# The filter's spectrum made on chip beside the first stage of batch 1, with the second stage lagging 13 steps

## The chip, the core and the metric

The kernel runs on one core of one Trainium2 chip. The metric is the device time of one execution in microseconds; three runs of the kernel before gave 908.36, 910.75 and 912.71, with a median of 910.75.

## What is computed

A causal long convolution by FFT, followed by a mixture of experts with soft slots. Everything is float32.

```python
# x (8, 5696, 128), h (5696, 128), phi (128, 32), w1 (8, 128, 1024), w2 (8, 1024, 128)
Xf = np.fft.rfft(x, n=2 * S, axis=1)
Hf = np.fft.rfft(h, n=2 * S, axis=0)
y  = np.fft.irfft(Xf * Hf[None], n=2 * S, axis=1)[:, :S].reshape(-1, D)
logits = y @ phi
d = softmax(logits, axis=0)                       # over all 45568 tokens
slot_input = (d.T @ y).reshape(E, 4, D)
slot_out[e] = np.maximum(slot_input[e] @ w1[e], 0) @ w2[e]
out = softmax(logits, axis=1) @ slot_out          # (45568, 128)
```

## The kernel before

The sequence of 5696 = 89 x 64 points is transformed by matmuls as a two-dimensional transform of 90 x 64. There are nine sequences: g = 0 is the filter h, g = 1 to 8 are the batches. Each goes through three stages, and DRAM scratch lies between the stages, since a stage needs another axis of the data on the partitions.

- **Stage A** (`stage_a`, lines 230 to 253). `load_x` (178) brings two chunks of 4 + 4 columns into one of two buffers `xc`; `fold` (209, line 217) makes sums and differences of near and far columns on POOL; PE multiplies by the table `s1` (241); ACT copies PSUM to a tile `fst` (243), of which there are four; the DMA that stores `fst` into `f` is kept back in `pending` and issued on SP's queue by `flush` (225). The low 60 frequencies of a chunk are done in every step, the high 30 of two chunks together in every odd step.
- **Stage B** (`stage_b1`, 275 to 314, and `stage_b2`, 316 to 352). A sequence has 12 units (NW). A unit loads a tile `gt` from `f` (`load_g`, 270), multiplies by `wt` on PE into the PSUM tile `bt` (284), and on VectorE multiplies by the filter's spectrum, `Hr` and `Hi` (304, 312). For the filter itself (g = 0) the multiplication is by the table `turn`, and line 308 writes `Hr` and `Hi` instead. `stage_b2` multiplies by `vt` (327) into `bz`, ACT copies to `zst` (332), and the store goes to `zm` or `zr`.
- **Stage C** (`stage_c1` to `stage_c6`, softmax and dispatch, 394 to 563). A pair of chunks T is loaded from `zm` and `zr` (374, 385), transformed by `im` and `ir` (412, 417), folded out, transposed (439), multiplied by phi (448), and taken through both softmaxes; `dispatch` (527) adds to the slots' accumulator.

The order is written by hand: the pools don't schedule. One loop over steps t interleaves the stages, and each engine gets its instructions in the order in which the loop names them. There are NJ = 8 chunks in a sequence. Stage A handles chunk t in step t, the filter in steps 0 to 7 and batch b in steps 8b to 8b + 7 (b from 1), until step 71. `units(t)` gives the stage-B units of a step, one in odd steps and two in even ones, with a lag:

```python
LAG_B, LAG_C = NJ + 1, 3 * NJ + 3      # 9 and 27
```

So filter B is in steps 9 to 16, B of batch 1 in steps 17 to 24, and stage C handles pair T from step 27 + 2T on. The loop ends at step 80 (`last_front`); the remaining pairs, the experts and the output follow in a tail. `prefetch` issues `gt` loads three units ahead. PSUM is split: four banks go round through `bank()`, two belong to `bt` and two to `bz`.

At the start VectorE sets `xc` and the stage-C buffers (176, 359 to 364), and ACT's queue issues the table loads and eight stores of zeros into `zr` (625), before its first copy. On SP's queue stand the filter's first loads, then the tables `wt` and `vt` (618, 619).

Of the kernel before, what the change touches and what calls it, by code (L numbers as in the profile page):

```python
# [11 lines left out]
F32 = mybir.dt.float32  # L12
AF = mybir.ActivationFunctionType
# [5 lines left out]
def transform_tables(S, N1, N2, CH, LOW, MAIN, XR):  # L19

    N, R1, HALF, P = N1 * N2, S // N2, N2 // 2, 2 * N2
    k1 = np.arange(N1)  # L30
    alpha = np.pi * (k1 + 0.5) / N1
    m1 = np.arange(R1) - (N1 - 1) / 2
    a1 = np.outer(m1, alpha)
    part = np.stack([np.cos(a1), -np.sin(a1), -np.cos(a1)], 1)
    s1 = np.zeros((P, 2, 3, N2 + HALF))
    for i, r in enumerate((slice(0, R1), slice(XR - R1, XR))):
        s1[r, i, :, 0:LOW] = part[:, :, 0:LOW]
        s1[r, i, :, N2:N2 + N1 - LOW] = part[:, :, LOW:]
    a0 = np.outer(alpha, np.arange(N1 // 2) + 0.5)
    part = np.stack([np.cos(a0), -np.sin(a0), -np.cos(a0)], 1)  # L40
    NP = N1 // 2
    im = np.zeros((2, MAIN, 2, N2))
    ir = np.zeros((2, 2, HALF, N2))
    for o in range(2):
        for c in range(2):
            im[o, :, c, 0:NP] = part[0:MAIN, o + c]
            ir[o, c, 0:N1 - MAIN, 0:NP] = part[MAIN:, o + c]
    k2 = np.arange(N2)
    omega = np.pi * (k1[:, None] + 2 * N1 * k2[None] + 0.5) / N
    m2 = np.arange(HALF) - (N2 - 1) / 2  # L50
    a2 = m2[None, :, None] * omega[:, None, :]
    w = np.concatenate([np.cos(a2), np.sin(a2)], 1)
    back = np.arange(N2).reshape(2, HALF).T.reshape(-1)
    NU = (NP + 1) // 2
    turn = (N1 - 1) / 2 * alpha[:, None] + (N2 - 1) / 2 * omega
    wq = np.zeros((2, N2, NP, N2))
    vq = np.zeros((2, N2, NU, 2, N2))
    tn = np.zeros((2, N2, 2, (NU + 1) // 2, 2, 2))
    for a in range(2):
        wq[a] = w[a::2].transpose(1, 0, 2)  # L60
        for q in range(NP):
            vq[q % 2, :, q // 2, a] = w[2 * q + a][back].T
            tn[q % 2, :, 0, q // 4, a, q // 2 % 2] = np.cos(turn[2 * q + a]) / N
            tn[q % 2, :, 1, q // 4, a, q // 2 % 2] = np.sin(turn[2 * q + a]) / N
    im, ir, wq, vq, tn = [t.reshape(P, *t.shape[k:]) for t, k in
                          ((im, 2), (ir, 3), (wq, 2), (vq, 2), (tn, 2))]
    return [np.ascontiguousarray(t, dtype=np.float32) for t in (s1, im, ir, wq, vq, tn)]
# [3 lines left out]
def kernel(  # L71
# [47 lines left out]
    t_s1, t_im, t_ir, t_w, t_v, t_turn = [  # L119
        nc.inline_tensor(t, f"tab_{n}").ap()  # L120
        for n, t in zip(("s1", "im", "ir", "w", "v", "turn"),
                        transform_tables(S, N1, N2, CH, LOW, MAIN, XR))]
    fd = [nc.dram_tensor(f"f_{g}", (N1, N2, 2, D), F32, kind="Internal").ap() for g in range(B + 1)]
# [26 lines left out]
    ypool = work.enter_context(tc.tile_pool(name="ypool", bufs=1))  # L150
    front = ExitStack()
# [6 lines left out]
    bpool = front.enter_context(tc.tile_pool(name="bpool", bufs=1))  # L158
# [5 lines left out]
    Hr = fconst.tile([P, NW, 2, 2, D], F32, name="Hr")  # L164
    Hi = fconst.tile([P, NW, 2, 2, D], F32, name="Hi")
# [9 lines left out]
    for t_ in xcs:  # L175
        nc.vector.memset(t_[:, :, :, :], 0.0)

    def load_x(m, halves=((0, 2 * CH),)):
# [3 lines left out]
        g, j = divmod(2 * m, NJ)  # L182
        if g == 0:
            src, blocks = h, ((0, R1 // 16 * 16), (R1 // 16 * 16, R1))
        else:
            r0 = min((g - 1) * R1, B * R1 - XR) * N2
            src, blocks = x.rearrange("b t d -> (b t) d")[r0:r0 + XR * N2], ((0, XR),)
        src = src.rearrange("(a n) d -> a n d", n=N2)
        t_ = xcs[m % len(xcs)]
# [19 lines left out]
    def fold(c):  # L209
        if c not in xs:  # L210
            return
        t_ = xs.pop(c)
        y_ = xf[c % len(xf)]
        i = CH * (c % 2)
        near, far = t_[:, 0, i:i + CH, :], t_[:, 1, ::-1, :][:, i:i + CH, :]
        for o in range(2):
            nc.gpsimd.tensor_tensor(out=y_[:, o, :, :], in0=near, in1=far,  # L217
                                    op=AL.subtract if o else AL.add)
        folded[c] = y_

# [6 lines left out]
    def columns(c, o):  # L227
        return folded[c][:, o, :, :].rearrange("p n d -> p (n d)")

    def stage_a(c, high):  # L230
# [7 lines left out]
        for q in range(2):  # L238
            p = bank()
            for i, (c_, o, m, cols) in enumerate(groups):  # L240
                nc.tensor.matmul(p[i * m:(i + 1) * m, :], s1[:, g // B, q + o, cols], columns(c_, o),  # L241
                                 start=True, stop=True)
            nc.scalar.activation(st[:, :, q, :],  # L243
                                 p[:, :].rearrange("p (n d) -> p n d", d=D), AF.Copy)
        k0, k1 = (LOW, N1) if high else (0, LOW)
        for i, (c_, o, m, _) in enumerate(groups):
            n0 = o * HALF + CH * (c_ % NJ)
            pending.append(partial(
                nc.sync.dma_start,
                out=fd[g][k0:k1, n0:n0 + CH, :, :].rearrange("k n c d -> k (n c d)"),  # L250
                in_=st[i * m:i * m + k1 - k0, :, :, :].rearrange("k n c d -> k (n c d)")))
# [12 lines left out]
    def load_g(u):  # L264
        if u >= (B + 1) * NW:
# [6 lines left out]
            in_=fd[g][8 * w:8 * w + 2 * n].rearrange("(q a) r c d -> (a r) q (c d)", a=2))  # L272
        gs[u] = t_

    def stage_b1(u):
        g, w, us = parts(u)
        t_ = gs.pop(u)
# [18 lines left out]
        for p_, H_ in (((pi[r, 0:k, :, :], turn[:, 1]), (pv, turn[:, 0])) if g == 0 else  # L296
                       ((pi[r, 0:k, :, :], Hi), (pv, Hr))):
            if g:
                h_ = H_[r, w].rearrange("p a o d -> p (a o) d") if m == 2 else H_[r, w, :, 0]
            else:  # L300
                h_ = (H_[r, w].rearrange("p a o -> p (a o)") if m == 2 else H_[r, w, :, 0]).unsqueeze(2)
                h_ = h_.broadcast_to([r.stop, k, D])
            h_ = h_.unsqueeze(2).broadcast_to([r.stop, k, 2, D])
            nc.vector.tensor_tensor(out=p_, in0=pv, in1=h_, op=AL.mult)  # L304
        if g == 0:
            for c, op_, H_ in ((0, AL.add, Hr), (1, AL.subtract, Hi)):
                h_ = H_[r, w, :, :, :].rearrange("p a o d -> p (a o) d") if m == 2 else H_[r, w, :, 0, :]
                nc.vector.tensor_tensor(out=h_, in0=pv[:, :, c, :], in1=pi[r, 0:k, 1 - c, :], op=op_)
            return
# [43 lines left out]
    ybufs = [ypool.tile([P, Q * CH, D + 1], F32, name=f"y{i}") for i in range(2)]  # L353
    zring = [(ypool.tile([P, 2, CH, 2, D], F32, name="zc"), ypool.tile([P, 2, CH, D], F32, name="zx"))]
    lt = ypool.tile([P, CH, 2, HP], F32, name="lt")
    dt = ypool.tile([P, CH, 2, HP], F32, name="dt")
    om, op = [ypool.tile([P, CH, D], F32, name=n) for n in ("om", "op")]
    yt = ypool.tile([D, Q * CH, 2, MH], F32, name="yt")
    nc.vector.memset(zring[0][1][:, :, :, :], 0.0)
    for t_ in (lt, dt):  # L360
        nc.vector.memset(t_[:, :, :, :], 0.0)
    nc.vector.memset(lt[HP:P, :, :, MH - 1:MH], -2.0 ** 127)
    for t_ in ybufs:
        nc.vector.memset(t_[:, :, D:D + 1], 1.0)
# [29 lines left out]
    def stage_c1(T, between=lambda: None):  # L394
        zt, zx = zs.pop(T)
        y_ = ybufs.pop(0)
        ybufs.append(y_)

# [36 lines left out]
    def stage_c2(T):  # L435
        for k in (3, 1, 0, 2) if tail else (3, 2, 1, 0):
# [8 lines left out]
    def stage_c3(T):  # L445
        p = bank()
# [8 lines left out]
    def column_max(T):  # L455
        mx = cpool.tile([P, 1], F32, name="mx", tag="mx")
        nc.vector.reduce_max(out=mx[:, :], in_=lt[:, :, :, 0:MH], axis=AX.XYZ)
# [13 lines left out]
    def stage_c4(T):  # L471

        p = bank()
# [3 lines left out]
        L = ypool.tile([P, Q, CH, NSL], F32, name="L", tag="L", bufs=2)  # L477
# [10 lines left out]
    def stage_c5(T):  # L488
        p = bank()
# [3 lines left out]
        d_ = ypool.tile([P, CH, P], F32, name="d", tag="d", bufs=1)  # L493
# [104 lines left out]
    LAG_B, LAG_C = NJ + 1, 3 * NJ + 3  # L598
# [4 lines left out]
    def units(t):  # L603
        g, i = divmod(t - LAG_B, NJ)
        if t < LAG_B or g > B:
            return []
# [3 lines left out]
    queue = [(u, t) for t in range(steps) for u in units(t)]  # L610
# [4 lines left out]
    load_x(0, ((0, CH), (CH, CH)))  # L615
    nc.scalar.dma_start(out=s1[:, :, :, :], in_=t_s1)
    load_x(1)
    nc.sync.dma_start(out=wt[:, :, :], in_=t_w)
    nc.sync.dma_start(out=vt[:, :, :, :], in_=t_v)
    nc.scalar.dma_start(out=phi[:, :], in_=moe_phi)  # L620
    nc.scalar.dma_start(out=turn[:, :, :, :, :], in_=t_turn)
    nc.scalar.dma_start(out=im[:, :, :], in_=t_im)
    nc.scalar.dma_start(out=ir[:, :], in_=t_ir)
    for i in range(8):
        nc.scalar.dma_start(
            out=zr[i // 4][i // 2 % 2, i % 2, N1 - MAIN:].rearrange("k (j r) d -> (k j) (r d)", r=2 * CH),
            in_=zring[0][1][0:4 * (HALF - N1 + MAIN), :, :, :].rearrange("p h n d -> p (h n d)"))
    fold(0)
    wait_b2 = []

    for t in range(last_front + 1):
# [23 lines left out]
        T, U, V, W, X = [pair(k) for k in (0, 2, 1, 3, 5)]  # L655
        if t < NA:
            stage_a(t, False)
            fold(t + 1)
        if t == last_front:
# [32 lines left out]
        else:  # L692
            if t % NJ == 0:
                prefetch(wait_b2[-1] + AHEAD if wait_b2 else AHEAD - 1)
# [238 lines left out]
```

## Time and profile before

| | |
|---|---|
| median of 3 runs | 910.75 us (908.36 to 912.71) |
| span of the profiled execution | 906.7 us; its own total time is not told, and the runs leave 2 to 6 us around the span |
| busy: PE, PEld, DVE, ACT, POOL | 757.3, 383.0, 601.1, 436.6, 399.9 us |
| DMA | 278.33 MB, mean 307 GB/s |
| `f` stores of all nine sequences | 144 of 240 KB and 144 of 120 KB |
| `gt` loads | 99 of 512 KB and 9 of 128 KB |

The profile is one execution seen by the hardware profiler. Its page shows the span in 40 slices of 22.7 us, one digit for each engine (the busy share in tenths), the clock that the throttle granted to PE, and the share and rate of the 16 DMA engines. "Windows" gives the same sums for stretches that one chooses, "timeline" the instructions in order of time with the idle time ahead of each and what released it, and "groups" the instructions of one line and shape with their busy time, mean duration in ns and idle time ahead. One float32 matmul instruction shows as two records. A row with SPq or ACTq is an instruction of the queue that issues a DMA, not its transfer.

### The profile page before, as it was taken

The page shows a single profiled execution, that of the slowest core. Times are in us where ns is not written, and L with a number is a line of the kernel's source. Part 1 is how long each engine was busy: PE and PEld are TensorE (multiplying, and loading weights), DVE is VectorE, ACT ScalarE, POOL GpSimd, SP SyncE. Part 2 cuts the span into 40 slices and gives each one's busy share as a digit, 9 for nine tenths or more (in the row PEclk, how much of TensorE's full clock was granted, in tenths as well). Part 3 has the DMA queues.
Part 4 walks back from the last instruction along what each step waited for, and adds up shares of the span by engine and source line. Part 5 has one row for each costly group of instructions (what it writes and reads, how often), then busy time and mean ns, then how long its engine had stood idle before and what let it go on. Part 6 is the DMA issues. An engine that isn't in the chain of part 4 may idle for free.

```text
span 906.7 us, 21292 instructions
## 1 busy us (share of the span) xinstructions
PE 757.3 (84%) x8308; PEld 383.0 (42%) x8308; DVE 601.1 (66%) x896; ACT 436.6 (48%) x880; POOL 399.9 (44%) x353
## 2 busy tenths in 40 slices
PE   5867687689989998998999999989888877767893
PEld 2222233234444443444444444435444434344882
DVE  2049876567778776777677787758778766653552
ACT  2423343345655565565556555645544444563441
POOL 4634424245656655655555566645332224651000
PEclk9889999989999999999899999989988888766865
DMA  8999999999999999999999999999988868540798
GB/s 264 314 312 342 321 362 290 307 369 357 320 298 375 347 322 337 353 315 291 360 354 331 312 366 348 324 329 331 294 252 293 267 199 341 186 164 1 296 405 332
DMA packets 170443, 278.33 MB, mean 307 GB/s; under 512 B 13543, under 2 KB 128231, under 8 KB 165135
## 3 DMA queue, kind: packets, MB, share of 16 engines
q1 hardware_dynamic: 169336, 275.74, 89.7%
q8 instruction: 66, 1.08, 0.5%
q10 hardware_dynamic: 1008, 1.25, 0.4%
q14 instruction: 33, 0.27, 0.1%
HBM read 147.94 MB, written 129.00 MB: 305 GB/s over the span
## 4 chain that ended last, share of the span: by engine, by line
PE 41%; DMA 32%; DVE 7%; ACT 7%; issue 6%; POOL 3%; SPq 2%; DVEq 0%; ACTq 0%; POOLq 0%
DMA gt<-f 9%; PE bt L284 8%; PE bank L241 7%; PE bz L327 7%; DMA zx<-zr 5%; DMA zc<-zm 5%; PE bank L412 4%; DMA out_dram<-o 4%; DMA f<-fst 4%; PE bank L417 3%; PE bank L439 3%; PE bank L448 2%; DMA zr<-zst 2%; ACT zst L332 2%; ACT fst L243 2%
## 5 line engine op out<-in xcount | busy, mean ns | idle before, releaser
L241 PE MATMUL bank<-x,s 128*32 128x512 f32 (+1 forms) x1152 | 216.5, 613 | 13.3 <-POOL x L217 8.2
L217 POOL TENSOR_TENSOR x<-xc 128x512 f32<-128x512 f32 x144 | 180.5, 1279 | 96.3 <-PE bank L241 77.8
L430 POOL TENSOR_TENSOR y<-y,op 128x512 f32<-128x512 f32 x64 | 77.6, 1212 | 227.6 <-DVE op L404 225.1
L284 PE MATMUL bt<-gt,wt 64*64 64x256 f32 x1620 | 123.3, 414 | 55.2 <-issue 27.1
L243 ACT ACTIVATE fst<-bank 128x512 f32<-128x512 f32 x216 | 123.0, 592 | 77.1 <-PE bank L241 53.5
L304 DVE TENSOR_TENSOR pi<-bt,Hi 128x1024 f32<-128x1024 f32 x96 | 112.9, 1176 | 65.1 <-PE bt L284 65.0
L332 ACT ACTIVATE zst<-bz 128x1024 f32<-128x1024 f32 x96 | 93.3, 972 | 109.8 <-PE bz L327 93.7
L312 DVE TENSOR_TENSOR yf<-bt,pi 128x512 f32<-128x512 f32 x192 | 119.3, 663 | 3.3
L284 PEld LDWEIGHTS bt<-gt,wt 64*64 64x64 f32 x1620 | 57.7, 140 | 135.7 <-issue 77.1
L304 DVE TENSOR_TENSOR bt<-bt,Hr 128x1024 f32<-128x1024 f32 x96 | 113.0, 1177 | 0.0
L327 PE MATMUL bz<-yf,vt 64*64 64x256 f32 x1440 | 109.3, 403 | 0.0
L241 PEld LDWEIGHTS bank<-x,s 128*32 128x32 f32 (+1 forms) x1152 | 54.0, 125 | 129.2 <-issue 91.3
L404 DVE TENSOR_TENSOR y<-bank,y 128x512 f32<-128x512 f32 x32 | 22.1, 692 | 97.2 <-ACT y L420 96.9
L327 PEld LDWEIGHTS bz<-yf,vt 64*64 64x64 f32 x1440 | 63.6, 143 | 25.4 <-issue 4.2
L512 POOL TENSOR_TENSOR L<-L,rs 128x512 f32<-128x512 f32 x32 | 33.5, 1048 | 87.2 <-DVE rs L511 43.7
L439 PE MATMUL bank<-ident,y 109*128 109x109 f32 x512 | 62.6, 272 | 8.8 <-ACT yt L441 8.8
L504 ACT ACTIVATE L<-L 128x512 f32<-128x512 f32 x32 | 20.2, 630 | 102.6 <-POOL L L501 102.6
L430 POOL TENSOR_TENSOR y<-y,om 128x512 f32<-128x512 f32 x54 | 63.9, 1183 | 2.1
L420 ACT ACTIVATE y<-bank 128x512 f32<-128x512 f32 x32 | 19.1, 596 | 93.0 <-PE bank L417 93.0
L439 PEld LDWEIGHTS bank<-ident,y 109*128 109x128 f32 x512 | 52.6, 148 | 20.4 <-POOL x L217 16.4
L412 PE MATMUL bank<-zc,im 64*64 64x512 f32 x480 | 60.8, 623 | 0.0
L441 ACT ACTIVATE yt<-bank 128x360 f32<-128x360 f32 x128 | 53.0, 483 | 6.2 <-PE bank L439 5.8
(101 smaller groups left out, 861.7 us busy)
## 6 DMA issues: line engine op xcount, KB each, us to landing
gt<-f SPq DMA_DIRECT2D x99, 512.0 KB
f<-fst SPq DMA_DIRECT2D x144, 240.0 KB
zm<-zst SPq DMA_DIRECT2D x128, 256.0 KB
zc<-zm SPq DMA_DIRECT2D x30, 1024.0 KB
xc<-in_x_dram SPq DMA_DIRECT2D x32, 768.0 KB
f<-fst SPq DMA_DIRECT2D x144, 120.0 KB
out_dram<-o SPq DMA_DIRECT2D x16, 1024.0 KB
zx<-zr SPq DMA_DIRECT2D x30, 512.0 KB
```

Source lines behind the costliest of these rows:

```text
L217: nc.gpsimd.tensor_tensor(out=y_[:, o, :, :], in0=near, in1=far, op=AL.subtract if o else AL.add)
L241: nc.tensor.matmul(p[i * m:(i + 1) * m, :], s1[:, g // B, q + o, cols], columns(c_, o), start=True, stop=True)
L243: nc.scalar.activation(st[:, :, q, :], p[:, :].rearrange("p (n d) -> p n d", d=D), AF.Copy)
L284: nc.tensor.matmul(bt[q * HP:(q + 1) * HP, a, o, :], wt[r, 2 * i + q, :], t_[r, 2 * o + q, :, :].rearrange("p c d -> p (c d)"), start=True ...
L304: nc.vector.tensor_tensor(out=p_, in0=pv, in1=h_, op=AL.mult)
L312: nc.vector.tensor_tensor(out=y_[r, 0:k, c, :], in0=pv[:, :, c, :], in1=pi[r, 0:k, 1 - c, :], op=op_)
L327: nc.tensor.matmul(bz[a * HP:(a + 1) * HP, q, o, :], vt[r, i, a, :], y_[r, a * m + o, :, :].rearrange("p c d -> p (c d)"), start=True, sto ...
L332: nc.scalar.activation(st[:, 0:m, 0:n, :].rearrange("p o q x -> p q o x"), bz[:, 0:n, 0:m, :], AF.Copy)
L412: nc.tensor.matmul(ps[o, c][h_ * HP:(h_ + 1) * HP, :], im[r, c, :], zt[r, h_, :, c, :], start=True, stop=False)
L430: eng.tensor_tensor(out=part_, in0=part(v, 0), in1=o_[:, :, :], op=sign)
L439: nc.tensor.transpose(p[:, i * TR:(i + 1) * TR], ys[T][0:TR, k * CH + i, 0:D], ident[0:TR, 0:TR])
L441: nc.scalar.activation(yt[:, k * CH:(k + 1) * CH, :, :], of_tokens(p), AF.Copy)
```

## The change

The filter no longer goes through DRAM. The loop starts at step 8, with stage A of batch 1, and the lags grow: `LAG_B` is 13 and `LAG_C` is 31, so that B of batch 1 is in steps 21 to 28, stage C starts at step 31, and `last_front` is step 84.

- All filter chunks are loaded at the start into buffers of their own (`hx`, in the space that `Hr` and `Hi` take later), on SP's queue among the first three loads of x and ahead of `wt` and `vt`. `fold_filter` makes the sums and differences on VectorE into `hf`, with the column index innermost.
- `filter_a`: 16 groups of 8 features in steps 11 to 16 (3, 3, 3, 3, 2, 2). Each is 32 matmuls with 32 columns of weights from `hf` and a moving table `sh` of 90 columns, into `bt` or `bz` by turns; VectorE copies the odd groups and ACT the even ones to `Fh`, a tile in SBUF.
- Filter B in steps 17 to 20, three units each, reads `Fh` instead of `gt`. ACT makes the products with one part of `turn` (four instructions of 256 elements a unit), and VectorE finishes `Hr` and `Hi` with eight instructions of 128 elements, in place of four instructions of 1024 and 512.
- The stage-C buffers become views of one tile, `ymain`, in the space of `Fh`. `open_y` allocates it at step 21, where POOL now sets it and ACT's queue issues the eight `zr` stores, ahead of that step's stage A.
- Stage A works on 96 partitions (XR) instead of 128, and `xc` is no longer cleared.

```diff
-    Hr = fconst.tile([P, NW, 2, 2, D], F32, name="Hr")
-    Hi = fconst.tile([P, NW, 2, 2, D], F32, name="Hi")
+    hx = [fconst.tile([P, n, 2, 2 * CH, D], F32, name=f"hx{i}", tag=k)
+          for i, (n, k) in enumerate(((3, "Hr"), (1, "Hi")))]
...
+    def fold_filter(c):
+        t_ = xs.pop(c)
+        i = CH * (c % 2)
+        near, far = t_[0:R1, 0, i:i + CH, :], t_[0:R1, 1, ::-1, :][:, i:i + CH, :]
+        for o, op_ in ((0, AL.add), (1, AL.subtract)):
+            nc.vector.tensor_tensor(out=hf[0:R1, o, :, CH * c:CH * c + CH].rearrange("p d n -> p n d"),
+                              in0=near, in1=far, op=op_)
+
+    HG = 2 * CH
+
+    def filter_a(k):
+
+        p = bps.tile([P, 2, 512], F32, name="fh", tag="bz" if k % 2 else "bt")
+        for i in range(HG):
+            for a in range(2):
+                for o in range(2):
+                    g = (2 * a + o) * HALF
+                    nc.tensor.matmul(p[g:g + HALF, i // CH, i % CH * N1:(i % CH + 1) * N1],
+                                     hf[0:R1, o, k * HG + i, :], sh[0:R1, o, a, :],
+                                     start=True, stop=True)
+        src = p[:, :, 0:CH * N1].rearrange("p b (i x) -> p x b i", i=CH)
+        dst = Fh[:, :, :, k * HG:(k + 1) * HG].rearrange("p k c (b i) -> p (k c) b i", b=2)
+        if k % 2:
+            nc.vector.tensor_copy(out=dst, in_=src)
+        else:
+            nc.scalar.activation(dst, src, AF.Copy)
...
-        t_ = gs.pop(u)
+        t_ = gs.pop(u) if g else Fh[:, 4 * w:min(4 * w + 4, NP), :, :]
...
+        if g == 0:
+            blocks = [(a, o) for a in range(2) for o in range(m)]
+            for i, (a, o) in enumerate(blocks):
+                nc.scalar.activation(pi[r, i, :, :], pv[:, i, :, :], AF.Copy,
+                                     scale=turn[r, 1, w, a, o:o + 1])
+            for i, (a, o) in enumerate(blocks):
+                for c, op_, H_ in ((0, AL.add, Hr), (1, AL.subtract, Hi)):
+                    nc.vector.scalar_tensor_tensor(
+                        out=H_[r, w, a, o, :], in0=pv[:, i, c, :], scalar=turn[r, 0, w, a, o:o + 1],
+                        in1=pi[r, i, 1 - c, :], op0=AL.mult, op1=op_)
+            return
...
+    def open_y():
...
+        all_ = ypool.tile([P, n], F32, name="ymain", tag="main")
...
+        nc.gpsimd.memset(yv["zx"], 0.0)
+        for i in range(8):
+            nc.scalar.dma_start(
+                out=zr[i // 4][i // 2 % 2, i % 2, N1 - MAIN:].rearrange(
+                    "k (j r) d -> (k j) (r d)", r=2 * CH),
+                in_=yv["zx"][0:4 * (HALF - N1 + MAIN)].rearrange("p h n d -> p (h n d)"))
+        for k in ("lt", "dt"):
+            nc.gpsimd.memset(yv[k], 0.0)
...
-    LAG_B, LAG_C = NJ + 1, 3 * NJ + 3
+    LAG_B, LAG_C = NJ + 5, 3 * NJ + 7
+    GH = dict(zip(range(NJ + 3, NJ + 9), (3, 3, 3, 3, 2, 2)))
+    UH = {LAG_B + NJ - 4 + i: (3 * i, 3 * i + 3) for i in range(4)}
...
+    load_x(NJ // 2, ((0, CH), (CH, CH)))
+    load_x(0)
+    load_x(NJ // 2 + 1)
+    for m in range(1, NJ // 2):
+        load_x(m)
     nc.sync.dma_start(out=wt[:, :, :], in_=t_w)
     nc.sync.dma_start(out=vt[:, :, :, :], in_=t_v)
...
-    fold(0)
+    fold(NJ)
+    for c in range(NJ):
+        fold_filter(c)
...
-    for t in range(last_front + 1):
+    for t in range(NJ, last_front + 1):
...
+        if t == LAG_B + NJ:
+            open_y()
         if t < NA:
             stage_a(t, False)
             fold(t + 1)
+        for _ in range(GH.get(t, 0)):
+            filter_a(left.pop(0))
+        if t == LAG_B + NJ - 4:
+            assert not left
+            first.close()
+            bpool = front.enter_context(tc.tile_pool(name="bpool", bufs=1))
+        while t < LAG_B + NJ and us:
+            slot_b()
```

## The prediction

> **What bounds the kernel now.** A step is one turn of the loop over t; A is the first stage (lines 241 and 243), B the second (284 to 332), C the rest. I began with the page's slices, which show that the bound differs by stage.
>
> ```profile
> PE   5867687689989998998999999989888877767893
> ...
> PEclk9889999989999999999899999989988888766865
> DMA  8999999999999999999999999999988868540798
> ```
>
> DMA stands at 9 for 28 slices in a row, so the change, which takes away traffic, is aimed at the busiest resource. Next I cut the span into stages with the windows view; the columns are the stretch, its length, busy us of PE, PEld, DVE, ACT and POOL, granted clock, DMA share, GB/s.
>
> ```profile
> 0.00:8.00 8.00, 0.00 (x0) 0.00 (x0) 5.58 (x8) 0.00 (x0) 1.82 (x8) 1.00 0.63 162
> 8.00:43.00 35.00, 29.66 (x128) 9.08 (x128) 0.00 (x0) 13.55 (x23) 21.26 (x18) 0.90 0.95 319
> 43.00:96.00 53.00, 39.55 (x322) 13.65 (x320) 37.01 (x42) 16.40 (x28) 24.82 (x20) 0.94 0.97 324
> 96.00:173.00 77.00, 57.82 (x600) 25.41 (x596) 54.47 (x64) 30.34 (x43) 24.85 (x20) 0.96 1.00 327
> 173.00:663.00 490.00, 449.08 (x5101) 213.85 (x5100) 362.93 (x550) 269.63 (x543) 260.92 (x222) 0.98 0.99 332
> 663.00:747.00 84.00, 66.06 (x768) 37.16 (x760) 63.09 (x97) 36.82 (x75) 27.09 (x24) 0.84 0.79 258
> ```
>
> The rows are: start; A of the filter (steps 0 to 7); B of the filter (8 to 16); B of batch 1 (17 to 26); all stages together (27 to 72); B and C without A (73 to 80). Up to 663 us DMA paces. Without A its share falls to 0.79, yet steps hardly shorten: z loads of steps 25, 57, 65, 73 and 79 are issued at 168.0, 500.8, 583.4, 663.2 and 724.4 us, so a step takes 10.4 us with A ((583.4-168.0)/40) and 10.2 without. There DVE (63 of 84 us) and PE at a 0.84 clock pace. So **DMA taken out late buys almost nothing; what counts is when C starts.** C starts at step 27, at 173.2 us, and in the changed kernel at step 31. The step count from there to the tail is 53 in both. I price the stretch up to C.
>
> **What goes.** Filter A and B through HBM: 5.9 MB written and 5.9 MB read, 8 steps of A, 12 units of filter B at 3.6 us of DVE (two of 1.22, two of 0.69, less overlap; the chain of waits shows them back to back from 73 to 94 us). The loop begins at step 8, and C's step 31 comes 23 steps later instead of 27.
>
> **What comes, step by step.** (1) *Start.* All four filter loads, wt and vt now stand ahead of the first f store. In the kernel before, the fifth fst tile waits for the first to be stored:
>
> ```profile
> 27.52 1.08 ACT L243 ACTIVATE fst<-bank 128x512 f32<-128x512 f32 x2 [7.09 <-DMA f<-fst]
> ```
>
> By then 6,744 KB had been queued (tables 448, zr 768, three filter loads 2,136, wt and vt 2,912, store 480): 260 GB/s counted from 1 us. After, it is 9,172 KB (tables 628, three x loads 2,304, four filter loads 2,848, wt and vt 2,912, store 480), so the store lands at 36 us. The fifth fst tile is step 11's, and in ACT's order it stands ahead of the copy that frees the transform's first bank. PE gets through A of steps 8 to 11 and two groups by about 30 us, then waits; step 11's copies (2 x 0.59), the bank copy (0.77), the third group and the rest of A end it at 41.5 us. fold_filter's 16 DVE operations lie under this: 0.69 each by line 312, 1.3 by line 430 in the tail, 11 to 21 us beside DVE's empty 0 to 43.
>
> (2) *The transform on PE.* 16 groups of 32 matmuls of 32x90, two records each. The nearest row is the dispatch, with weights of the same width and 129 columns, here in the timeline:
>
> ```profile
> 418.98 1.10 PE L527 MATMUL bank<-y,d 128*32 128x129 f32 x32
> ```
>
> That is 34 ns a record back to back; line 852 (128 columns, 128 records in 3.7 us) gives 29. Scaled by columns the floor is 20, unscaled the ceiling 34; I take 26, near the short row, since issue doesn't shrink with columns: 64 x 26 = 1.65 us a group (1.3 to 2.2). The Trainium skill ("TensorE: Matmul & The Clock Gate", section "Wait — 56ns, not 53.3ns?") gives a start-to-start floor of about 25 ns however short the matmul, by which a group would be 1.6 us; no row of this trace has so short a matmul in that form. Copies out (720 elements, between 592 and 1025 ns on ACT by lines 243 and 332, 690 and 1222 on DVE by lines 308 and 304) run under the next group, by the two tags. If that cover were gone they would add 16 x 0.85 = 14 us. Steps 12 to 16 hold seven blocks of A at 1.87 us and 13 groups: 13.1 + 21.5 = 34.6. After PE's long wait the first work runs at half clock, as before (a bt block takes 1.98 instead of 1.09 us at 669.8, after 3.08 us idle): +2. Step 17 then starts at **78 us** (70 to 88).
>
> (3) *Filter B, steps 17 to 20.* Twelve units from the chip: 8 matmuls (1.09 us), four ACT scalings of 256 elements, eight DVE operations of 128.
>
> ```profile
> L332 ACT ACTIVATE zst<-bz 128x256 f32<-128x256 f32 x8 | 3.1, 383 | 3.0 <-PE bz L327 2.1 <-DMA f<-fst 0.9
> ...
> L532 DVE SCALAR_TENSOR_TENSOR acc<-acc,dn,bank 128x129 f32<-128x129 f32 x31 | 8.3, 268 | 3.4 <-PE bank L527 3.4
> ```
>
> DVE: 92 x 0.26 = 24 us; ACT: 46 x 0.38 = 17.5. Two banks alternate, so a step's third unit waits until DVE is done with the first: 0.5 of ACT and 2.1 of DVE after that one's matmuls, less the second unit's 1.1 meanwhile, leave 1.5 of PE waiting. PE: six blocks of A 11.2, units 12.5, waits 4 x 1.5: **30 us** (26 if DVE never pauses, 36 if ACT's fst copies hold the scalings). DMA needs only 14 (4 x 1.1 MB), so it can't be what paces. Step 21 starts at 108. It does what step 17 did, which began at 95.6:
>
> ```profile
> 95.55 1.94 PE L241 MATMUL bank<-x,s 128*64 128x512 f32 x8
> ...
> 173.15 1.94 PE L241 MATMUL bank<-x,s 128*64 128x512 f32 x8
> ```
>
> So **+12.5 us**. The ten steps from there to C move the same bytes at a DMA share of 1.0, 77.6 us in both.
>
> (4) *open_y at step 21.* Memsets on POOL ahead of fold(22) are hidden (about 3 us; the fold is needed some 8 us later). The eight zr stores stand in ACT's queue ahead of step 21's fst copies; they took 7.77 us at 6.2 us, and now the first waits for the memset and others for gt and x landings. Behind them wait fst, hence PE's banks, hence f and z stores. PE has some 5 us of other work: +4 (0 to 8).
>
> (5) *The rest.* fold and A's matmuls over 96 partitions: durations go by the free size, nothing. Four steps of C lose A: 4 x 0.2 = -1. The stage-C buffers become views of one tile; stage C waits on nearly the same engines at each instruction in the two built programs: nothing. One w1 load is repeated (0.5 MB, beside a DMA share under 0.8): nothing.
>
> Sum: 12.5 + 4 - 1 = **+15.5**. The profiled span is 906.7; its own total isn't told, but the runs (908.36 to 912.71) leave 2 to 6 us around it, so I add to the median: 910.75 + 15.5 = 926.
>
> **Rivals.** *DMA paces the head too* (ends faster). If copies and matmuls hide, bytes set step 21: first loads 8.9 MB, six more x loads 4.7, f stores of 13 steps 9.3, three gt 1.6: 24.5 MB at 315 GB/s and 2 us of start are 80 us against 95.6, so 895. It decides if steps 11 to 20 average under 4.5 us; A alone takes 2.8 on PE. For it: the 0.95 share from 8 to 43. Against it: three groups add 5 us to a step whose bytes need 3.5. Beside it the Trainium skill ("Perfetto Trace Analysis", section "Identifying the Most-Contended Engine") says to improve the most-contended engine, which is DMA here. 0.17. *The pieces cancel*: groups at 1.3 us, units at 26, no stall at step 21, a start stall 6 us shorter: 15.5-4-4-4-6 gives 908; 0.10. *Views of one tile order stage C*: 1 us in each of 32 pairs gives 958; for it, one name where twelve were, against it the equal waits: 0.05. *The transform runs at half clock*: there the dispatch takes 1.83 us for 32 records (673.4 us), 57 ns each; 16 x 64 x 31 ns is 32 us more, 958; it needs waits between the groups long enough to drop the clock; against it, stage A lies between them: 0.04. The same page and section of the Trainium skill gives 62 ns a matmul where the sequencer decodes in microcode, by which the sum would be some 37 us more; the rows at 29 and 34 ns speak against that. My forecast holds 0.64.
>
> **Chances and range.** About 0.5% (4.6 us) is what a measurement of this kernel can tell from no change. Faster 0.17, same 0.10, slower 0.73. The forecast's own bounds add to 908 and 945 (groups +7, units +6, stall +4, +2 of start); to leave out no more than 0.2 I reach down to 902.
>
> **What would show it.** Right: PE idle near 30 to 38 us; 26 ns a record; step 21's A near 108 us; a hole in PE and ACT just after; C from about 189; steps of 10.4 us later. Wrong: step 21 before 96 us (the DMA rival), stage-C pairs over 21 us (the views), or steps without A under 9.5 us, which would make the removed traffic worth something late.

## The result, and the profile after

| | before | after |
|---|---|---|
| median of 4 runs | 911.39 us (908.36 to 912.71) | 935.03 us (934.22 to 939.0) |
| ratio after / before | | 1.0267 (95%: 1.0232 to 1.0302) |
| span of the profiled execution | 906.7 us | 933.7 us (its own time is 935.59) |
| DMA | 278.33 MB | 267.35 MB |

The change made the kernel 2.7% slower, though it moves 11 MB less. Single runs of the kernels below spread by up to 36 us, and the longer ones show a lower granted clock in their records; ratios leave the disturbed runs out.

These are the slices of after's page, as the prediction showed them for before (PE's clock and the DMA share):

```profile
PE   5598768767997999999799989999778877667893
...
PEclk9679888997999999999999989999888888878865
DMA  9955389999999999999999999999789848460698
```

The change shows in the first six digits of the DMA line: 9 9 5 5 3 8, where before had 8 and then 9s. From there on the two lines are much alike. The windows view of after cuts that stretch finer. Its columns are the stretch, its length, busy us of PE, PEld, DVE, ACT and POOL, then granted clock, DMA share and GB/s:

```profile
25.00:50.00 25.00, 15.02 (x220) 8.68 (x223) 7.43 (x9) 4.31 (x7) 5.94 (x5) 0.59 0.87 285
50.00:75.00 25.00, 23.50 (x674) 17.43 (x676) 4.54 (x5) 8.46 (x13) 6.48 (x6) 0.87 0.52 145
75.00:100.00 25.00, 19.92 (x348) 9.18 (x336) 9.36 (x31) 14.88 (x32) 9.95 (x8) 0.93 0.55 147
100.00:125.00 25.00, 17.81 (x138) 6.36 (x140) 16.64 (x64) 13.88 (x33) 4.10 (x5) 0.79 0.49 150
```

From 50 to 125 us DMA works at half its share and PE is busy, or waits at a low clock. Nothing that was taken off DMA can shorten this stretch.

I read the time by the start of a step, which is the start of its first matmul of stage A:

| | before | after | forecast of after |
|---|---|---|---|
| step 12 (after only) | | 46.3 | 41.5 |
| step 17 of after | | 82.7 | 78 |
| batch 1 enters B (before's step 17, after's 21) | 95.6 | 123.2 | 108 |
| C starts (before's step 27, after's 31) | 173.2 | 203.0 | 189 |
| from there to the end of the span | 733.6 | 730.7 | 1 less |

So +27.7 us in the head, +2.1 in the ten steps up to C, and -2.8 in all the rest give the +27.0 between the spans. The medians differ by 23.6.

**The start**, in after's timeline (line 246 is `filter_a`, 276 stage A's matmul, 254 ACT's copy to `Fh`, 278 the copy to `fst`, 234 the sums on VectorE):

```profile
30.70 0.51 PE L246 MATMUL fh<-sh,hf 89*32 89x90 f32 x2 [6.57 <-DVE hf L234]
31.57 4.88 PE L246 MATMUL fh<-sh,hf 89*32 89x90 f32 x126 [0.37 <-DVE hf L234]
40.37 2.63 PE L246 MATMUL fh<-sh,hf 89*32 89x90 f32 x64 [3.91 <-ACT Fh L254]
42.77 7.25 PE L276 MATMUL bank<-x,s 96*32 96x512 f32 x24
49.95 7.14 PE L246 MATMUL fh<-sh,hf 89*32 89x90 f32 x192
...
58.89 3.93 PE L246 MATMUL fh<-sh,hf 89*32 89x90 f32 x192
```

```profile
19.40 12.12 DVE L234 TENSOR_TENSOR hf<-hx 89x512 f32<-89x512 f32 x12 [2.93 <-DMA hx<-in_h_dram]
```

```profile
38.57 1.08 ACT L278 ACTIVATE fst<-bank 128x512 f32<-128x512 f32 x2 [15.82 <-DMA f<-fst]
39.54 0.78 ACT L254 ACTIVATE Fh<-fh 128x720 f32<-128x720 f32 x1
```

PE stops twice: 6.57 us for the sums on VectorE, whose last one ends at 31.5 us, and 3.91 us for the copy to `Fh`, which stands behind the `fst` copy that waited for the first store. Then three groups of the transform take 7.14 us; nine microseconds later the same three groups take 3.93. That factor is the granted clock: 0.52 from 50 to 57 us, 1.00 from 59 to 62.6. PE was busy all the time from 40.4 to 57.0 us, and still the clock stayed at 0.50 to 0.52.

**The filter's units**, in the same timeline (line 319 is stage B's first multiply, 338 the product that writes `Hr` and `Hi`):

```profile
84.59 1.96 PE L319 MATMUL bt<-Fh,wt 64*64 64x256 f32 x32
89.66 1.09 PE L319 MATMUL bt<-Fh,wt 64*64 64x256 f32 x16 [3.11 <-DVE Hi L338]
90.69 5.46 PE L276 MATMUL bank<-x,s 96*32 96x512 f32 x24
96.07 1.96 PE L319 MATMUL bt<-Fh,wt 64*64 64x256 f32 x32
101.14 1.98 PE L319 MATMUL bt<-Fh,wt 64*64 64x256 f32 x16 [3.11 <-DVE Hi L338]
```

Two units run, the third waits 3.11 us for VectorE to be done with the first one's bank, and what comes behind the wait is often at a lower clock: 5.46 us for 24 records that take 3.77 at 62.6 us, 1.98 for a block that takes 1.09. ACT and VectorE of the first unit show where the 3.11 comes from (line 334 is ACT's scaling):

```profile
85.75 3.03 ACT L334 ACTIVATE pi<-bt,turn 128x256 f32<-128x256 f32 x8 [0.45 <-PE bt L319]
```

```profile
87.36 0.35 DVE L338 SCALAR_TENSOR_TENSOR Hr<-bt,turn,pi 128x128 f32<-128x128 f32 x1 [3.59 <-ACT pi L334]
```

The four scalings of a unit take 3.03 / 2 = 1.5 us. VectorE's first product begins only when all four are done, 1.61 us after the first began, though it needs only one of them.

### The profile page after: what moved, and what is told of

Same layout as the page of the kernel before. It is cut to its first block, busy times and chain, and to the rows that moved or that the text cites. A ratio compares the mean times of both kernels' runs of the same rounds, so it can differ in the third digit from the quotient of the medians.

```text
span 933.7 us, 23047 instructions
## 1 busy us (share of the span) xinstructions
PE 772.0 (83%) x9204; PEld 404.9 (43%) x9204; DVE 601.6 (64%) x956; ACT 448.2 (48%) x910; POOL 383.0 (41%) x343
## 2 busy tenths in 40 slices
DMA packets 162852, 267.35 MB, mean 286 GB/s; under 512 B 12876, under 2 KB 121932, under 8 KB 157538
## 4 chain that ended last, share of the span: by engine, by line
PE 54%; DMA 25%; ACT 7%; issue 6%; DVE 3%; POOL 2%; SPq 1%; ACTq 0%; DVEq 0%; POOLq 0%
PE bank L276 12%; PE bt L319 10%; PE bz L363 7%; DMA ymain<-zr 6%; DMA gt<-f 6%; PE bank L468 5%; DMA out_dram<-o 4%; PE bank L473 4%; PE bank L496 3%; PE fh L246 2%; PE bank L506 2%; PE bank L587 2%; DMA ymain<-zm 2%; DMA f<-fst 2%; ACT zst L368 2%
## 5 line engine op out<-in xcount | busy, mean ns | idle before, releaser
L486 POOL TENSOR_TENSOR ymain<-ymain 128x512 f32<-128x512 f32 x116 | 137.6, 1196 | 232.7 <-DVE ymain L460 228.2
L225 POOL TENSOR_TENSOR x<-xc 96x512 f32<-96x512 f32 x128 | 161.3, 1284 | 127.4 <-PE bank L276 102.1
L276 PE MATMUL bank<-x,s 96*32 96x512 f32 (+1 forms) x1024 | 199.8, 640 | 11.2 <-POOL x L225 9.3
L319 PE MATMUL bt<-gt,wt 64*64 64x256 f32 x1440 | 112.3, 423 | 41.5 <-issue 30.7
L460 DVE TENSOR_TENSOR ymain<-bank,ymain 128x512 f32<-128x512 f32 x63 | 43.2, 686 | 93.9 <-ACT ymain L476 93.9
L276 PEld LDWEIGHTS bank<-x,s 96*32 96x32 f32 (+1 forms) x1024 | 48.6, 129 | 116.3 <-issue 85.6
L496 PE MATMUL bank<-ident,ymain 109*128 109x109 f32 x496 | 60.6, 272 | 7.6 <-ACT ymain L498 7.5
L468 PE MATMUL bank<-ymain,im 64*64 64x512 f32 x480 | 60.3, 618 | 0.0
L496 PEld LDWEIGHTS bank<-ident,ymain 109*128 109x128 f32 x496 | 51.1, 149 | 18.8 <-POOL x L225 13.8
L498 ACT ACTIVATE ymain<-bank 128x360 f32<-128x360 f32 x128 | 53.1, 482 | 9.0 <-PE bank L496 8.6
L473 PE MATMUL bank<-ymain,ir 26*64 26x512 f32 x480 | 36.1, 659 | 18.7 <-DMA ymain<-zr 18.7
```

The source lines that it names most:

```text
L225: nc.gpsimd.tensor_tensor(out=y_[0:XR, o, :, :], in0=near, in1=far, op=AL.subtract if o else AL.add)
L276: nc.tensor.matmul(p[i * m:(i + 1) * m, :], s1[0:XR, g // B, q + o, cols], columns(c_, o), start=True, stop=True)
L319: nc.tensor.matmul(bt[q * HP:(q + 1) * HP, a, o, :], wt[r, 2 * i + q, :], t_[r, 2 * o + q, :, :].rearrange("p c d -> p (c d)"), start=True ...
L468: nc.tensor.matmul(ps[o, c][h_ * HP:(h_ + 1) * HP, :], im[r, c, :], zt[r, h_, :, c, :], start=True, stop=False)
L473: nc.tensor.matmul(p[h_ * HP:(h_ + 1) * HP, :], ir[r, :], zx[r, h_, :, :], start=False, stop=True)
L486: eng.tensor_tensor(out=part_, in0=part(v, 0), in1=o_[:, :, :], op=sign)
```

## The experiments

Two theories stood against each other. **Chain:** the head is now set by a chain of PE, ACT and VectorE through the transform and the filter's units, so each of the two adds its time to step 21 and the bytes saved are worth nothing. **DMA:** the loads and stores of the head pace it as before, and the new work lies beside them.

| | profiled span | step 12 | 17 | 21 | 31 | median | ratio to before |
|---|---|---|---|---|---|---|---|
| after | 933.7 | 46.3 | 82.7 | 123.2 | 203.0 | 935.03 | 1.0267 |
| e1, no transform | 908.0 | 39.4 | 56.0 | 97.9 | 177.5 | one run, 909.84 | |
| e2, no units | 908.6 | | 81.3 | 93.3 | 181.7 | one run, 910.35 | |
| e7, neither | 882.6 | | 55.8 | 69.0 | 160.5 | one run, 884.50 | |
| e4, tables late | 933.8 | 44.7 | 80.0 | 124.3 | 204.5 | 936.33 | 1.0217 (1.0152 to 1.0283) |
| e5, by block | 935.3 | | 79.6 | 131.9 | 212.9 | 941.51 | 1.0327 (1.0289 to 1.0364) |
| e8, units spread | 932.8 | 46.1 | 87.3 | 116.7 | 202.2 | 929.03 | 1.0222 (1.0160 to 1.0284) |

In the kernels with the old lag of 9 the units are in steps 13 to 16, batch 1 enters B at step 17 and C starts at 27:

| | profiled span | step 13 | 17 | 27 | median | ratio to before |
|---|---|---|---|---|---|---|
| e3, lag 9 | 932.0 | 73.3 | 120.7 | 209.6 | 918.29 to 953.8 | |
| e6, e3 to e5 together | 938.8 | 71.1 | 125.7 | 210.3 | 942.53 | 1.0317 (1.0282 to 1.0352) |
| e9, lag 9, units spread | 923.6 | 75.5 | 102.0 | 188.6 | 923.85 | 1.0175 (1.0128 to 1.0223) |
| e10, e9 and another start | 922.6 | 75.9 | 105.5 | 196.3 | 929.88 | 1.0211 (1.0123 to 1.0299) |
| e11, e9 and zeros early | 913.5 | 73.3 | 103.3 | 180.3 | 922.35 | |
| e12, e11, tables late, groups later | 933.6 | 89.4 | 119.7 | 197.1 | 927.06 | 1.0143 (1.0069 to 1.0216) |

### e1, e2 and e7: leave a part out

e1 leaves out the filter's transform (`Fh` holds a constant), e2 the filter's units (`Hr` and `Hi` hold constants), e7 both; the rest stands as in after.

```diff
-            filter_a(left.pop(0))
+            left.pop(0)
```
```diff
-        while t < LAG_B + NJ and us:
-            slot_b()
+        if t < LAG_B + NJ:
+            us = []
```

> The 16 groups of the transform are left out (Fh is set to a constant on VectorE instead). Theory 'chain' (the new work stands in line on PE, ACT and DVE ahead of stage C, and DMA has slack there): steps 11 to 16 fall to stage A's own pace once the first f store has landed at 38.6 us, so step 17 starts near 57 us instead of 82.7, and the span falls by about 25 us to 908. Theory 'bytes' (DMA paces the head): step 17 stays within 4 us of 82.7 and the span within 4 of 934. Theory 'stage C got slower by its merged tile': span within 4 us of 934, and a longer stretch from step 31 to the end.

> The 12 filter units of stage B are left out (Hr and Hi are set to a constant on VectorE). 'Chain': steps 17 to 20 last 14 us (four steps of A at 3.5, the pace of their bytes) instead of 40.5, span 934 - 26 = 908. 'Bytes': span within 4 us of 934. If only the waits of PE on VectorE inside the units cost, and not the units' own matmuls, the gain is 12 us (four waits of 3.1).

> Both left out: no transform and no filter units, loads and sums of the filter remain. 'Chain': the gains add until the bytes become the bound: 24.5 MB up to step 21 at 315 GB/s puts step 21 near 80 us instead of 123.2, span about 890. 'Bytes': span within 4 us of 934.

The span falls by 25.7 us without the transform, by 25.1 without the units, and by 51.1 without both. Each part adds its time, as a link of a chain does. That the two gains add up to within 0.3 us is partly luck: there is one run of each, and by the start of C the gains are 25.5, 21.3 and 42.5 us, which is 4 less together than one by one. The rest lies behind the start of C, where the seven kernels with a lag of 13 have the same work and took 722 to 731 us in their profiled runs.

e7 also shows where the DMA theory would hold. These are two of its windows, and the first block of batch 1's B:

```profile
25.00:50.00 25.00, 11.43 (x50) 3.14 (x42) 16.78 (x10) 6.76 (x12) 9.70 (x8) 0.66 0.97 318
50.00:75.00 25.00, 21.81 (x103) 6.08 (x102) 0.00 (x0) 10.12 (x19) 19.77 (x21) 1.00 0.95 325
```

```profile
82.79 1.99 PE L319 MATMUL bt<-gt,wt 64*64 64x256 f32 x16 [10.78 <-DMA gt<-f]
```

With the new work gone DMA stands at 0.95 to 0.97 in these windows, and that block waits 10.78 us for its load. So up to the start of C, what the change takes away is worth 173.2 - 160.5 = 12.7 us, and what it puts in costs 203.0 - 160.5 = 42.5. Over the whole span it is 906.7 - 882.6 = 24.1 and 51.1, but the parts of these that lie behind the start of C, 11.4 and 8.6 us, can't be told from the spread of single runs.

### e3: the lag of before

Back to lags of 9 and 27, with four groups in each of steps 9 to 12.

```diff
-    LAG_B, LAG_C = NJ + 5, 3 * NJ + 7
-    GH = dict(zip(range(NJ + 3, NJ + 9), (3, 3, 3, 3, 2, 2)))
+    LAG_B, LAG_C = NJ + 1, 3 * NJ + 3
+    GH = dict(zip(range(NJ + 1, NJ + 5), (4, 4, 4, 4)))
```

> Stage B's lag goes back to 9 steps and C's to 27; the 16 groups stand in steps 9 to 12 (four each), the filter units in 13 to 16. The same work, but four steps of stage A less ahead of stage C. 'Chain': PE saves 11 us of A and its waits ahead of C, step 17 near 103 us and about 914 us in all (-20). If the steps of A ahead of C were hidden (the rival on the lag), nothing changes: 935 within 4.

Four runs gave 918.29, 934.11, 951.69 and 953.8, in the order of their granted clocks (0.909, 0.881, 0.862, 0.861), so no ratio can be given. The profiled run is the second of them (934.11), so its timeline shows how that execution lost time, and not what the fastest one did:

```profile
80.26 1.98 PE L319 MATMUL bt<-Fh,wt 64*64 64x256 f32 x16 [3.11 <-DVE Hi L338]
82.17 7.25 PE L276 MATMUL bank<-x,s 96*32 96x512 f32 x24
```

The same wait of 3.11 us, and behind it 24 records of stage A in 7.25 us instead of 3.77. Steps 13 to 16 take 47.4 us here. What the lag by itself costs stays open. The fastest run, 918.29, has no profile; it is near the 914 that was expected, and 16 us under the shortest run of after, and beside it the kernel before ran from 906.93 to 918.79. With the units spread, the lag of 9 is 5 us faster than that of 13 (e9 and e8 below: medians of 923.85 and 929.03, and their runs don't overlap).

### e4: the tables for B later

`wt` and `vt` (2,912 KB) go behind the first stores, out of the way of the first `f` store.

```diff
-    nc.sync.dma_start(out=wt[:, :, :], in_=t_w)
-    nc.sync.dma_start(out=vt[:, :, :, :], in_=t_v)
...
+            if t == NJ + 2:
+                flush()
+                nc.sync.dma_start(out=wt[:, :, :], in_=t_w)
+                nc.sync.dma_start(out=vt[:, :, :, :], in_=t_v)
```

> The tables wt and vt (2,912 KB) are loaded behind the first f stores, at step 10, instead of ahead of them. 'Chain', with the start's stall made by the order of the queue: the first f store lands some 11 us sooner (27 instead of 38.6 us), ACT's wait of 15.8 us goes, the third group follows the filter's sums (31.5 us) at once, and step 12 starts near 42 instead of 46.3: -4 to -6 us, 930. Rival (PE waits for the filter's sums alone): 0, 935.

The store did land earlier: the `fst` copy that began at 38.57 us now begins at 30.61. Step 12 moved by only 1.6 us, and the median is no lower than after's. PE's line of this kernel says why:

```profile
33.56 7.63 PE L246 MATMUL fh<-sh,hf 89*32 89x90 f32 x189 [1.39 <-DVE hf L234]
```

PE still waits for the sums. They end at 33.5 us here instead of 31.5 (the twelve that begin at 19.3 us take 14.2 us instead of 12.1), and the groups behind them run at 40 ns a record, half clock. So the 3.91 us for the copy are gone, and 2 of them are lost again: under the wait that I had named lay another one.

### e5: hand VectorE each block as it comes

Each scaling writes a buffer of its own, so that VectorE may begin after the first of the four.

```diff
-            for i, (a, o) in enumerate(blocks):
-                nc.scalar.activation(pi[r, i, :, :], pv[:, i, :, :], AF.Copy,
+                pb = bpool.tile([P, 4, 2, D], F32, name="pb", tag="yf" if i > 1 else "zst",
+                                bufs=2 if i > 1 else 3)[:, 0]
+                nc.scalar.activation(pb[r, :, :], pv[:, i, :, :], AF.Copy,
```

> In the filter units each ACT scaling has a tile of its own and VectorE follows it block by block, instead of waiting for all four. 'Chain', the wait of PE for the third unit (3.1 us, four times) made of four scalings and eight VectorE operations: each wait shrinks by about 1.2, in all -5 us, 930. Rival (ACT or the two banks pace the units): 0, 935.

It went the other way: steps 17 to 20 took 52.3 us instead of 40.5. ACT's timeline shows the two engines taking turns:

```profile
83.76 0.47 ACT L335 ACTIVATE pb<-bt,turn 128x256 f32<-128x256 f32 x1 [0.68 <-DVE Hi L338]
84.91 0.47 ACT L335 ACTIVATE pb<-bt,turn 128x256 f32<-128x256 f32 x1 [0.68 <-DVE Hi L338]
86.06 0.84 ACT L335 ACTIVATE pb<-bt,turn 128x256 f32<-128x256 f32 x2 [0.68 <-DVE Hi L338]
```

Each scaling now waits for VectorE's products of the block before, although both only read `bt` and write elsewhere. The last row holds two scalings: a unit's fourth, and behind it without a wait the next unit's first, which reads another tile. So in this program the readers of one PSUM tile are held to the order of the code. A unit takes four turns of about 1.2 us, which is more than the 1.5 + 2.1 us of the unsplit form. The edit made a new wait; it doesn't test the old one.

### e6: e3, e4 and e5 together, and all loads of the filter first

```diff
+    for m in range(NJ // 2):
+        load_x(m)
...
-    load_x(0)
```

> Lag 9, tables late, block by block, and the four filter loads ahead of the loads of x, so that the sums end near 21 instead of 31.5 us. 'Chain': the gains add: step 17 near 85 us, and 903 in all, which is under the kernel before (911) by more than 0.5%; 895 to 912. Rival: the early gains overlap, since each removes a wait that another one covers, and it comes out no lower than lag 9 alone, about 914.

Stage A started at 22.9 us instead of 8.0, since x's loads now stood behind the filter's four, and e5's new wait was in it. It came out no faster than after (1.0317 against 1.0267, with intervals that overlap), far from the 903 that was expected.

### e8: two units ahead of a step's stage A, one behind it

The same 12 units, but PE has a block of stage A to do between the second and the third. These lines stand ahead of `stage_a(t, False)`, and so does the opening of the units' pool; the loop behind it finds one unit left.

```diff
+        if t in UH:
+            slot_b()
+            slot_b()
```

> The same work as the changed kernel in another order: in steps 17 to 20 two filter units stand ahead of the low block of stage A and the third behind it, so that PE has a block of A while VectorE finishes the first unit. Theory 'chain with an idle PE' (a wait of 3.1 us per step, and half clock in the blocks behind it): the four steps shrink from 40.5 to about 30 us (two banks, each held 4.8 us by matmuls, ACT and VectorE, give 2.4 us a unit, 29 at least), total about 925. Rival (ACT and VectorE pace the units whatever PE does meanwhile): 40 us and 935.

Within the steps it did what it should. Step 17 now begins with two units, at 85.44 us (the 87.3 of the table is the block of stage A behind them), and from there to step 21 it took 31.3 us instead of 40.5, with waits of 1.1 to 1.8 us and a granted clock of 1.00 from 75 to 100 us. But C starts only 0.8 us earlier, and the profiled span moved by 0.9 us. (This is the longest of four runs. The median is 6 us lower than after's, but the kernel before ran 4 us lower beside it too, and the intervals of the two ratios overlap.) The next step took the gain back. ACT's queue and PE, in e8's timelines (line 411 is the stores of zeros):

```profile
117.86 9.40 ACTq L411 DMA_DIRECT2D zr<-ymain  x8
127.36 2.06 ACT L278 ACTIVATE fst<-bank 128x512 f32<-128x512 f32 x4 [9.72 <-DMA zr<-ymain]
```

```profile
128.11 3.68 PE L276 MATMUL bank<-x,s 96*64 96x512 f32 x8 [6.60 <-POOL x L225]
```

Eight stores hold ACT's queue for 9.4 us. The `fst` copies stand behind them, PE has no bank, and its next block after 6.60 us of idling runs at half clock (3.68 instead of 1.94). In after the same stores took 7.01 us and PE waited just 1.75 for them. The row names POOL as the releaser, but PE's block starts 0.15 us after the first of the four `fst` copies is over (127.36 + 0.60), and in e9's trace the same wait has ACT's name.

### e9 and e10: the lag of 9 with the units spread

e9 is e3 with e8's edit; e10 also takes e4's and e6's order of loads.

> Lag 9 with the units spread in the same way. 'Chain with an idle PE': the four steps with units fall from 47 us (lag 9 alone) to about 32, and PE stays at full clock behind them; about 905, at or a little under the kernel before. Rival (the saved steps of A were only filling waits that now stand empty): 918 or more, as the undisturbed run of lag 9 alone.

> As before it, with the filter's loads ahead of x and the tables wt and vt behind the first f stores; no tiles of their own for the scalings. 'Chain with an idle PE': the sums end near 26 instead of 31.5 us, and step 9's groups start that much sooner: 5 us under lag 9 with spread units, about 900. Rival (stage A then starts 15 us later, at 22.9 us as in the run with all edits, and eats the gain): equal to lag 9 with spread units within 4.

e9 and e3 differ only in the place of two `slot_b()` calls a step and of the pool that they need. From the first unit (72.35 us) to step 17 it takes 29.6 us in e9; steps 13 to 16 take 47.4 in the profiled run of e3. The place of the calls alone isn't shown to be worth that, since e3's fastest run, 918.29, lies under all four of e9 (921.68 to 925.73). e9 then loses 5.86 us of PE to the same eight stores, and C starts 86.6 us after step 17 where before needs 77.6:

```profile
112.64 3.68 PE L276 MATMUL bank<-x,s 96*64 96x512 f32 x8 [5.86 <-ACT fst L278]
```

e10 started its stage A at 23.1 us and gained nothing by that.

### e11: the zeros at the start

e9, with the stores of zeros issued before the loop, from `Fh`, which is still empty then.

```diff
+    nc.vector.memset(Fh[:, 0:4, :, :], 0.0)
+    for i in range(8):
+        nc.scalar.dma_start(
+            out=zr[i // 4][i // 2 % 2, i % 2, N1 - MAIN:].rearrange("k (j r) d -> (k j) (r d)", r=2 * CH),
+            in_=Fh[0:4 * (HALF - N1 + MAIN), 0:4, :, :].rearrange("p h n d -> p (h n d)"))
```

> Lag 9 with spread units, and the eight zr stores go out at the start, from a zeroed piece of Fh, instead of standing in ACT's queue when stage C's buffers are opened; the memset of zx goes with them. In lag 9 with spread units the two steps behind the opening take 23.6 us (17 to 19) where the kernel before takes 16.3, with PE idle 5.9 us for an fst copy. Theory 'the zero stores hold ACT': the ten steps 17 to 27 go from 86.6 to about 79, and the time from 924 to 916. Rival (the first loads of B hold it, and the stores only lie beside): 86 and 924; and 0.77 MB more at the start may cost up to 3 us.

Steps 17 to 26 fell from 86.6 to 77.0 us, which is before's 77.6. The hole has gone from PE's timeline:

```profile
110.07 1.09 PE L319 MATMUL bt<-gt,wt 64*64 64x256 f32 x16
110.95 1.07 PE L363 MATMUL bz<-yf,vt 64*64 64x256 f32 x16
115.01 1.51 PE L319 MATMUL bt<-gt,wt 64*64 64x256 f32 x16 [2.98 <-issue]
```

Four runs gave 913.36, 915.69, 929.02 and 937.72, with granted clocks of 0.905, 0.898, 0.883 and 0.876, beside a median of 910.3 (905.27 to 914.46) for the kernel before. The first is the lowest time of any version that does all of the work, and it isn't below before's median.

### e12: e11 with the tables late and the groups in steps 10 to 12

```diff
-    GH = dict(zip(range(NJ + 1, NJ + 5), (4, 4, 4, 4)))
+    GH = dict(zip(range(NJ + 2, NJ + 5), (5, 6, 5)))
```

> As e11, and the tables wt and vt behind the first f stores, and the groups in steps 10 to 12 (5, 6, 5), so that stage A's blocks of steps 9 and 10 fill PE's wait for the filter's sums. 'Chain': two blocks of A less behind the sums, 4 us at full clock and 7 at half: 910, beside the kernel before at 907 to 911. Rival (the wait for f's stores or loads of x comes in its place): equal to e11 within 4.

It was meant to be the best and wasn't. The profiled run is the longest of its four (935.88; the others gave 918.92, 925.84 and 928.28), so it doesn't explain the median. In it the ten steps up to C took 77.4 us, as in e11, but step 13 starts at 89.4 us instead of 73.3. A window shows the reason:

```profile
50.00:75.00 25.00, 25.00 (x480) 18.25 (x480) 2.73 (x3) 5.30 (x9) 4.95 (x4) 0.50 0.24 64
```

PE was busy for all of these 25 us, and the clock stayed at 0.50; 384 records of the transform took 14.63 us there, 38 ns each. The Trainium skill ("TensorE: Matmul & The Clock Gate", section "What's actually happening") says that full speed comes after about 3.4 us of sustained work. This window doesn't agree: 25 us of work were not enough. Nor does after's trace, with its 16 us at 0.50 to 0.52.

## Why the prediction came out as it did

The forecast was slower at 926, in a range of 902 to 945, and 935.03 is in it. The mechanism held: DMA didn't pace the head, and what counted was when C starts. The size did not: 15.5 us were forecast and 23.6 measured, and C started at 203.0 us and not at 189. Between the spans it is 27.0; the five terms below were off by +4.8, -0.1, +10.5, -1.9 and -1.8, which is what the forecast lacks. One by one:

1. *Start, 41.5; measured 46.3.* The wait that ends the start was named rightly: the copy to `Fh` stood behind an `fst` copy that waited for the first store. The store landed at 38.6 us instead of 36 (at the sum's own rate, counted from 1 us, it would have been 37). Behind it the third group and the rest of A ran at half clock, 2.6 and 3.6 us where the sum had 1.65 and 1.9. Together these make the 4.8 us. Another wait lay under this one. I costed the sums at nothing, since VectorE had nothing else to do, but the transform waits for the last of them. They took 1.0 us each (1.02 to 1.04 in most rows, inside the 0.69 to 1.3 that I gave), they couldn't begin before their loads landed, at 12.67 and 19.40 us, and PE waited 6.57 us for them. In after the later wait covers that, and e4 shows that without the late store they would still hold. An idle engine hides only what nobody waits for.
2. *Transform, 26 ns a record; steps 12 to 16 in 36.6 us with the allowance; measured 36.4.* This is two errors that cancel. At full clock the records took 3.93 / 192 = 20.5 ns, the floor that I had scaled by columns, so a group is 1.31 us. By the Trainium skill's start-to-start floor of about 25 ns ("TensorE: Matmul & The Clock Gate", section "Wait — 56ns, not 53.3ns?") it would have been 1.6; this row lies below that. At half clock three groups took 3.2 us more than at full. So the 13 groups needed 17.0 us instead of 21.5, and what was saved there went to half clock, 3.2 us in these groups and 1.8 in a block of A (2 had been allowed for all of it), and to a wait of 1.5 us at 71.6.
3. *Units, 30 us; measured 40.5.* **This is the term that was mis-sized.** PE's own work was right (11.3 us of stage A and 12.5 of units). I let VectorE begin 0.5 us after a unit's matmuls; it began after all four scalings, some 1.6. The rows between 82.7 and 123.2 us sum to 12.3 us of waiting for `Hi` where I had 4 x 1.5 = 6, and blocks at a low clock lost 4.9 more: 11.3 + 12.5 + 12.3 + 4.9 = 41.0, against 40.5. e8 takes away the order that makes the wait, and the term falls to 31.3. How much belongs to the wait and how much to the clock was not separated by a run, as the one brings the other.
4. *open_y, +4; the ten steps measured +2.1.* The units' lateness probably left the DMA less to do by then; no run tests that. When the units got faster, the ten steps took 85.5 us (e8) and 86.6 (e9), 8 to 9 over before's 77.6, and e11 shows that it was the stores in ACT's queue: without them the ten steps took 77.0.
5. *The rest, -1; measured -2.8.* From C on, after needs 730.7 us and before 733.6, so neither a large gain from the missing traffic nor a loss to the merged views shows. Finer than that it can't be read, since the same work took 722 to 731 us in the kernels with a lag of 13.

The rivals: *DMA paces the head* needs a head like that of e7, and after has a DMA share of 0.49 to 0.55 from 50 to 125 us. *The pieces cancel* had the groups right (1.3 us) and the units wrong (26). *Views order stage C*, which would cost 32 us, is out by point 5. *The transform at half clock* came true for six of the sixteen groups in after (at 31.6 to 57 us), and for most of them in e12.

Of the signs that the prediction named, PE did stand idle around the first groups, from 24 to 31 and from 36 to 40 us. The 26 ns a record, step 21 near 108 us and C near 189 did not come, and the hole in PE behind step 21 was 1.75 us.

What stays open: why the clock stays at half through 25 us of steady work in e12 and 16 in after, why the same kernel runs at a mean clock of 0.861 one time and 0.909 another (e3), and what the lag alone costs. No version here that does all of the work beats the kernel before.

## What to carry to other kernels

Taking bytes off the busiest resource pays only where that resource still ends the stage; leave out the added work in an experiment (as e7 did) and you see the gain and the cost apart, here 12.7 and 42.5 us up to the start of C. When work is moved onto an engine because it is idle there, ask who waits for the last piece: twelve units and sixteen sums were each short, and each stood at the head of PE's queue. And when a repair shows its full effect in its own steps but not in the profiled span (e8), look at the very next step: another wait was standing there under cover.

## What the runs showed of the hardware

- Behind a wait of 3.11 us on PE, what followed ran at as little as half speed: 1.98 us instead of 1.09 (after, 101.1 us), 7.25 instead of 3.77 (e3, 82.2 us). It wasn't so every time: the block at 89.66 us behind the same wait took 1.09, and the low clock came one block later. A shorter wait was followed by it too: behind 1.76 us the block took 1.93 us in e8 (at 103.56) and 1.99 in e11 (at 88.78), but 1.09 in e9 (at 90.48).
- Half speed can last while PE is busy throughout (e12, 50 to 75 us, granted clock 0.50; after, 40.4 to 57.0 us, 0.50 to 0.52).
- Records of 32 weight columns by 90 moving columns, with four outputs side by side on the partitions, ran at 20.5 ns each at a granted clock of 1.00 (after, 58.89 us) and at 38 ns at 0.50 (e12, 50.93 us).
- The eight stores on ACT's queue held that queue, and every ACT instruction behind them, for 7.01 us in after, 8.71 in e9 and 9.40 in e8; over all runs it was 4.6 (e6) to 9.4 us.
